# Softmax weights turned by DMA transposes for nine of twelve head pairs, and full-row norm matmuls

## The chip, the cores and the metric

The kernel runs on one core of a Trainium2 chip. The metric is the device time of one execution in microseconds (us), the median of several runs. The engines are named as the profile names them: PE (TensorE; PEld is its weight load), DVE (VectorE), ACT (ScalarE), POOL (GpSimd) and SP (SyncE, from whose queue all DMA transfers are issued).

## The reference

Causal attention, then a gated layer, then a second layer with two products. All arrays are float32.

```python
# q, k, v: (2, 12, 448, 64)
scores = q @ k^T / 8, masked above the diagonal
attn = softmax(scores)                       # max subtracted, sum + 1e-9
x = (attn @ v), heads joined                 # (896, 768)
xn = x / sqrt(mean(x * x) + 1e-6) * rms_g
x = (silu(xn @ w_gate) * (xn @ w_val)) @ w_out      # d_ff 1536
a, b = x @ w1, x @ w2                        # 1024 wide
return ((a * b) @ w3) @ w_out2               # (896, 768)
```

## The kernel before

**The plan.** The kernel does not issue its instructions as it builds them. Every piece of work is given to `add` (line 75) with an engine, a planned cost in us, the keys that it reads and writes, and a priority; some carry an alternative engine (`alt`). `schedule` (line 104) is a list scheduler with these costs: it holds the time at which each of PE, ACT, DVE, POOL and SP comes free, takes at each step the ready work of best priority, and lets the first free of the allowed engines have it. `order` (line 209) runs it eight times, each time with priorities taken from a schedule of the same work backwards, and keeps the shortest plan. The instructions are then issued in the plan's order, and each engine runs its own in that order. The constants at the top (TP, WP0, PO and so on, BIAS, THETA) are first priorities and the willingness to hand work to another engine. A DMA is planned as time on SP plus 2.0 us until it has landed (`LAT`).

**The stages.** Attention works on twelve pairs of heads (`pair`, line 525; six per batch, `p` counts them from 0 to 11). Beside it PE computes W' = w3 times the last weights (`w_prime`, line 487), 384 matmuls of 384 columns which only the last stage needs. After each batch comes `norm` (line 651). The layers after it use seven block products instead of eight (`wino`, line 777), on operands split into a float16 high part and a bfloat16 rest ("hi" and "lo"), with three matmuls per product of two split operands. Their weights arrive through `fetch` (line 446) and are split by `halve` (line 468).

**One pair.** The scores of two heads go to PSUM, four token tiles of 128, 128, 128 and 64 rows; `soft` (line 550) has DVE add the mask and find the maximum (line 552) and ACT take the exponential (line 556). The weights of tiles 0 to 2 lie in `pA`, one buffer of 128 x 768 float32 per head, those of the last tile of both heads in `pB` (128 x 512). For the product with the values they must lie the other way round, and split. That is `turn` (line 587): four PE transposes of 128x128 float32 into one PSUM bank (line 592), an ACT copy of the bank to float16 (line 595), and a DVE subtraction that leaves the rest as bfloat16 (line 597). Three turns fill `tA`, one fills `tB`: four turns a pair, 48 in all. Then `pv` (line 614) multiplies the turned parts with the split values, three matmuls of 65 or 64 columns per block, and DVE scales the result by the reciprocal sum into `x4s` (line 638). The buffers: `qs` three, `pA` three, `pB` two, `tA` and `tB` two each; weight loads (`st`) four.

**The norm.** DVE multiplies the identity by each token's factor (`diag`, line 661). For each of six head pairs, PE multiplies `x4` by it (line 672): three token tiles of 128 rows, and the last with only its 64 rows. An ACT copy with the gain follows (line 677), then the splitting.

The splitting helpers are `hi_part` (line 437: a copy on ACT, or else DVE or POOL) and `lo_part` (line 442: a subtraction on DVE, or else POOL). The PE matmuls of all stages stand on line 482.

Of the kernel before, what the change touches and what calls it, by code (L numbers as in the profile page):

```python
# [9 lines left out]
F16 = mybir.dt.float16  # L10
BF16 = mybir.dt.bfloat16
# [29 lines left out]
TP = 17.8003  # L41
WP0 = -253.0822
WPS = 51.892
GVS = 4.2731
OS = 5.0631
AS = 4.1976
FS = -1.7478
PO = dict(dq=71.6219, dv=1.9008, vh=22.6565, vl=32.9822, sc=-23.6522, s3=-41.3333, hA=-61.8192, hl=29.4612,
    hB=-32.8733, pv=17.37, sq=-46.6736, nm=20.7661, wm=29.3375, ww=-33.8468, wx=26.0812, g=-0.9384,
    a=-36.9422, o=12.4298, f=-33.5642, gm=-18.8521, e=9.4561, ae=-40.4366, y=-26.7884, t1=30.9235,  # L50
    mx=16.587, dw=4.4531)
# [3 lines left out]
BIAS = {"dve": 16.6032, "pool": 54.8731, "act": 110.9515}  # L55
THETA = 0.4938
# [216 lines left out]
def fused_kernel(ctx: ExitStack, tc, qk, v, g, wgv, wo, wab, w3t, wout, out):  # L273
# [82 lines left out]
    vl_r = Ring("att", "vl", 2, [P, NT * GH, D], F16)  # L356
    zero = view("zero", [P + 252], F16)
# [123 lines left out]
    def mm(*a, **k):  # L481
        nc.tensor.matmul(*a, **k)  # L482
# [42 lines left out]
    def pair(b, gi):  # L525
# [33 lines left out]
        def scores(i, outs, keys, pr):  # L559
# [7 lines left out]
            add("pe", (2 if i < 3 else 1) * (0.1 + w * 0.00082), f, r=[kqs], w=keys, prio=pr, rows=0.5)  # L567
# [19 lines left out]
        def turn(blocks, dst, kd, r, pr):  # L587
# [5 lines left out]
            add("pe", 4 * 0.109, f, r=["ident", *r], w=[kp], prio=pr)  # L593
# [6 lines left out]

        order = [(i, j, kb) for i in range(3) for j in range(GH) for kb in range(i + 1)]
        where = {x: c for c, x in enumerate(order)}
        for c in range(0, 12, 4):
# [3 lines left out]
        turn([pB[:, kb * P:kb * P + P] for kb in range(4)], [tB[:, h, :, 0:P] for h in range(2)], ktB, [kpB], t0 + PO["hB"])  # L607

        for j in range(GH):
# [4 lines left out]
            def pv(i, o=o, j=j):  # L614
                n = 3 * (i + 1)
                k = 0
                for kb in range(i + 1):
                    if i < 3:
                        c = where[i, j, kb]
                        lh, ll = tA[:, 0, c], tA[:, 1, c].bitcast(BF16)  # L620
# [7 lines left out]
            for i in range(NT):  # L628
                kt = {ktA + (where[i, j, kb] // 4,) for kb in range(i + 1)} if i < 3 else [ktB]
                add("pe", 3 * (i + 1) * 0.0286, lambda pv=pv, i=i: pv(i), r=[  # L630
                    *(k + (h,) for k in sorted(kt) for h in range(2)), kvh, kvl], w=[ko], prio=pr)
# [19 lines left out]
    def norm(b):  # L651
# [13 lines left out]
        for gi in (0, 3, 1, 4, 2, 5):  # L665
# [3 lines left out]
            def f(x4=x4, ps=ps):  # L669
                for i in range(NT):  # L670
                    n = ROWS[i]
                    mm(ps[:, i * P:i * P + n], x4[:n, i], diag[:n, i, :n], start=True, stop=True)

            add("pe", 4 * S / 2400.0, f, r=["diag"] + [kx4 + (j,) for j in range(GH)], w=[kp], prio=pr)
# [256 lines left out]
```

## Time and profile before

| | |
|---|---|
| median of 3 runs | 555.97 us (555.76 to 556.53) |
| the profiled execution | 554.84 us |
| its span, first to last instruction | 553.1 us |
| PE busy | 539.6 us (98%) |
| DVE busy | 497.6 us (90%) |
| ACT busy | 343.0 us (62%) |
| POOL busy | 232.8 us (42%) |
| mean granted clock of PE | 0.996 |

The profile is one execution, taken by the hardware profiler. An engine's busy time counts its instructions and not its waiting. PE's matmuls are pipelined and their ends are modelled, so a busy PE is not PE at its peak. The chain of waits starts at the last instruction and goes back, at each step, to what released it, or to the instruction before it on its engine.

### The profile page before, as it was taken

Reading aid. Unit: us, or ns where it says so; the run is one execution under the profiler, and the core shown is the slowest. Engines: PE = TensorE matmul, PEld = TensorE weight load, DVE = VectorE, ACT = ScalarE, POOL = GpSimd, SP = SyncE. Lnnn points to the kernel's source line nnn. Section 1 sums busy time; section 2 is a strip of 40 time slices with the busy share of each in tenths; the row PEclk is TensorE's granted clock in tenths of the full one; section 3 lists DMA queues with packets and bytes.
Section 4 is the critical chain, followed back from the end, with each engine's and each line's share of the span. In section 5 each row is a group of like instructions: output and inputs, shape, how many; then the busy total and the mean of one; then the engine's idle time right before and its main releaser. Section 6 shows DMA issues by size and latency. Waiting matters only on the chain.

```text
span 553.1 us, 9446 instructions
## 1 busy us (share of the span) xinstructions
PE 539.6 (98%) x3586; PEld 304.0 (55%) x3586; DVE 497.6 (90%) x919; ACT 343.0 (62%) x500; POOL 232.8 (42%) x198
## 2 busy tenths in 40 slices
PE   7799999999999999999999999999999999999997
PEld 5465666677667555555555555555555555455553
DVE  6898999889987999999999999999659999999943
ACT  5898869778755767676746677857435516533310
POOL 5545225164120475569674744132112476353300
PEclk8999999999999999999999999999999999999999
DMA  8887646723130232535231447536103311000121
GB/s 278 272 281 245 181 136 180 259 89 94 32 115 1 65 118 104 173 109 176 97 132 60 120 165 253 204 116 228 58 0 119 111 59 58 0 1 0 42 92 69
DMA packets 17470, 67.59 MB, mean 122 GB/s; under 512 B 2064, under 2 KB 3600, under 8 KB 17424
## 3 DMA queue, kind: packets, MB, share of 16 engines
q1 hardware_dynamic: 17424, 66.99, 36.3%
q8 instruction: 28, 0.46, 0.3%
q14 instruction: 18, 0.15, 0.1%
HBM read 64.23 MB, written 2.75 MB: 121 GB/s over the span
## 4 chain that ended last, share of the span: by engine, by line
PE 75%; DVE 15%; DMA 4%; issue 3%; ACT 2%; SPq 0%; DVEq 0%; ACTq 0%
PE bank L482 71%; PE bank L592 3%; DVE arena L443 3%; DMA st<-in_w3t 3%; DVE arena L795 3%; DVE arena L478 2%; DVE st L478 2%; DVE cv L464 2%; DVE cv L457 1%; DMA arena<-in_qk 1%; ACT st L460 1%; DVE arena L552 1%; PE bank L428 1%; DVE arena L439 0%; DVE st L462 0%
## 5 line engine op out<-in xcount | busy, mean ns | idle before, releaser
L482 PE MATMUL bank<-arena 128*128 128x448 f16 (+8 forms) x2976 | 446.2, 316 | 8.0 <-DVE arena L552 2.1
L482 PEld LDWEIGHTS <-arena 128*128 128x128 f16 x3048 | 250.8, 98 | 215.2 <-issue 11.6
L460 ACT ACTIVATE st<-st 128x768 uint16<-128x768 uint16 (+2 forms) x73 | 119.7, 1665 | 26.7 <-DVE cv L457 23.4
L795 DVE TENSOR_TENSOR arena<-bank,arena 128x448 f32<-128x448 f32 x161 | 92.6, 612 | 13.9 <-PE bank L482 13.3
L444 POOL TENSOR_TENSOR arena<-cv,arena 128x384 bf16<-128x384 f32 (+2 forms) x42 | 61.5, 1468 | 44.8 <-ACT arena L438 43.9
L444 POOL TENSOR_TENSOR arena<-arena 128x448 bf16<-128x448 f32 x32 | 51.2, 1613 | 65.1 <-ACT arena L438 65.0
L464 DVE SCALAR_TENSOR_TENSOR cv<-st,cv 128x768 int32<-128x768 int32 (+2 forms) x84 | 75.5, 905 | 1.8 <-ACT st L460 1.4
L482 PE MATMUL bank<-xs,arena 128*128 128x448 f16 x360 | 72.5, 352 | 0.0
L438 ACT ACTIVATE arena<-arena 128x448 f16<-128x448 f32 x73 | 40.6, 573 | 38.6 <-DVE arena L478 33.1
L457 DVE TENSOR_SCALAR cv<-st 128x768 int32<-128x768 int32 (+2 forms) x84 | 54.4, 654 | 8.0 <-DMA st<-in_w3t 4.1
L438 ACT ACTIVATE arena<-cv 128x384 f16<-128x384 f32 (+2 forms) x56 | 37.3, 673 | 29.8 <-PE bank L482 16.6
L443 DVE TENSOR_TENSOR arena<-st,arena 128x1536 bf16<-128x1536 f32 (+1 forms) x25 | 45.8, 1834 | 0.0
L478 DVE TENSOR_TENSOR arena<-arena 128x448 f32<-128x448 f32 x60 | 39.3, 667 | 6.9 <-ACT arena L841 4.5
L556 ACT ACTIVATE arena<-arena 128x256 f32<-128x256 f32 (+3 forms) x84 | 42.0, 519 | 5.5 <-DVE arena L552 5.3
L440 POOL TENSOR_SCALAR arena<-cv 128x384 f16<-128x384 f32 (+2 forms) x26 | 21.5, 828 | 55.8 <-DVE cv L464 28.4
L552 DVE CUSTOM_DVE_ANT_0 arena<-bank,arena 128x128 f32<-128x128 f32 (+3 forms) x84 | 36.3, 443 | 3.3 <-PE bank L482 2.5
L438 ACT ACTIVATE arena<-st 128x1536 f16<-128x1536 f32 (+1 forms) x21 | 29.0, 1383 | 15.4 <-DVE st L478 9.2
L597 DVE TENSOR_TENSOR arena<-bank,arena 128x512 bf16<-128x512 f32 x48 | 32.7, 684 | 6.2 <-ACT arena L595 6.0
L443 DVE TENSOR_TENSOR arena<-cv,arena 128x768 bf16<-128x768 f32 (+2 forms) x42 | 35.0, 833 | 0.9 <-POOL arena L440 0.7
L595 ACT ACTIVATE arena<-bank 128x512 f16<-128x512 f32 x48 | 29.0, 607 | 10.9 <-PE bank L592 10.5
L479 POOL TENSOR_TENSOR arena<-arena 128x448 f32<-128x448 f32 x20 | 27.5, 1378 | 16.0 <-DVE arena L795 14.7
L482 PEld LDWEIGHTS bank<-arena 64*128 64x128 f32 (+2 forms) x288 | 26.0, 179 | 14.9 <-issue 4.7
(69 smaller groups left out, 359.9 us busy)
## 6 DMA issues: line engine op xcount, KB each, us to landing
st<-in_wgv SPq DMA_DIRECT2D x24, 768.0 KB, 4.3
st<-in_wab SPq DMA_DIRECT2D x16, 768.0 KB, 4.7
st<-in_wo SPq DMA_DIRECT2D x12, 768.0 KB, 4.5
st<-in_w3t SPq DMA_DIRECT2D x16, 512.0 KB, 5.1
st<-in_wout SPq DMA_DIRECT2D x16, 384.0 KB, 3.5
arena<-in_qk SPq DMA_DIRECT2D x12, 448.0 KB, 4.4
arena<-in_v SPq DMA_DIRECT2D x12, 256.0 KB, 3.2
out_t<-arena SPq DMA_DIRECT2D x12, 224.0 KB, 1.9
```

Source lines behind the costliest of these rows:

```text
L438: add("act", act_us(n), lambda: nc.scalar.activation(hi, src, AF.Copy), r=r, w=w, prio=prio, alt=(("dve", dve2_us(n), lambda: nc.vector.te ...
L443: add("dve", dve_us(n), lambda: nc.vector.tensor_tensor(lo, src, hi, op=ALU.subtract), r=r, w=w, prio=prio, port=True, alt=(("pool", pool_ ...
L444: port=True, alt=(("pool", pool_us(n), lambda: nc.gpsimd.tensor_tensor(lo, src, hi, op=ALU.subtract)),))
L457: add("dve", dve2_us(n), lambda: nc.vector.tensor_scalar(cv, hi, 3, 0x3FFFFFFF, op0=ALU.logical_shift_left, op1=ALU.bitwise_and), r=[ks], ...
L460: add("act", ACT_TOP * n - 0.08, lambda: nc.scalar.activation(b[:, :, 2], b[:, :, 1], AF.Copy, scale=1.0 / 8192, bias=-8191.0 / 16384), w= ...
L464: add("dve", dve_us(n), lambda: nc.vector.scalar_tensor_tensor(cv, hi, -0x3FFFFFF9, cv, op0=ALU.bitwise_and, op1=ALU.bitwise_or), r=[ks], ...
L478: add("dve", dve_us(n), lambda: nc.vector.tensor_tensor(out, a, b, op=op), port=True, alt=(("pool", pool_us(n) + 0.1, lambda: nc.gpsimd.te ...
L482: nc.tensor.matmul(*a, **k)
L552: add("dve", dve_us(w), lambda: nc.vector.tensor_tensor_reduce(out=sc[:, :w], in0=ss[:, :w], in1=m, scale=-CSC, scalar=3.0e38, op0=ALU.add ...
L556: add("act", act_us(w) + 0.1, lambda: nc.scalar.activation(dst, sc[:, :w], AF.Exp, bias=mx[:, c:c + 1], scale=-1.0), r=[ksc, kmx + (c,)], ...
L597: add("dve", dve_us(512), lambda: nc.vector.tensor_tensor(dst[1].bitcast(BF16), src, dst[0], op=ALU.subtract), r=[kp, kd + (0,)], w=[kd + ...
L795: add("dve", dve_us(S), lambda: nc.vector.tensor_tensor(dst, ps, y, op=ALU.add), r=[kp, ky], w=[kd], prio=p)
```

## The change

Pairs 3 to 11 (`DA` for the three tiles of A, `DB` for the last tile) no longer turn their weights on PE. The weights are split first, as they lie: `hi_part` and `lo_part` write a float16 and a bfloat16 half side by side into a new buffer (`hA`, two of 128 x 2 x 768; `hB`, one of 128 x 2 x 512), and one DMA transpose on the SP queue turns both halves into `tA` or `tB`. That is three transfers a pair: one for A per head (768 columns, two halves), one for B (512 columns, two halves). Pairs 0 to 2 keep the four turns on PE. The order of the blocks in `tA` differs for the new way, so `pv` takes other indices and waits for other keys.

The norm's last token tile is multiplied over all 128 rows of `x4` and `diag`; the rows from 64 on meet zeros of `diag`.

The planned PE costs of scores, turns and the norm are changed, and the constants of the first priorities, BIAS and THETA have new values (in part left out below), so the order of the whole program can differ.

```diff
-TP = 17.8003
-WP0 = -253.0822
-WPS = 51.892
+TP = 28.0521
+WP0 = -244.6493
+WPS = 48.9793
...
-BIAS = {"dve": 16.6032, "pool": 54.8731, "act": 110.9515}
-THETA = 0.4938
+BIAS = {"dve": 17.4016, "pool": 80.0945, "act": 139.3857}
+THETA = 0.4843
+
+DA, DB = range(3,12), range(3,12)
...
+    hA_r = Ring("att", "hA", 2, [P, 2, 768], F16)
+    hB_r = Ring("att", "hB", 1, [P, 2, 512], F16)
...
-            add("pe", (2 if i < 3 else 1) * (0.1 + w * 0.00082), f, r=[kqs], w=keys, prio=pr, rows=0.5)
+            add("pe", 0.12 + 2 * (0.1 + w * 0.00082), f, r=[kqs], w=keys, prio=pr, rows=0.5)
...
-            add("pe", 4 * 0.109, f, r=["ident", *r], w=[kp], prio=pr)
+            add("pe", 4 * 0.109 + 0.04, f, r=["ident", *r], w=[kp], prio=pr)
...
+        def send(n, h, kh, src, ks, dst, kd, us, pr):
+            hi_part(n, h[:, 0], src, ks, [kh + (0,)], pr)
+            lo_part(n, h[:, 1].bitcast(BF16), src, h[:, 0], ks + [kh + (0,)], [kh + (1,)], pr + PO["hl"])
+            add("sp", us, lambda: nc.sync.dma_start_transpose(out=dst, in_=h.rearrange("p a c -> p (a c)")),
+                r=[kh + (0,), kh + (1,)], w=kd, prio=pr - 30)
+
         order = [(i, j, kb) for i in range(3) for j in range(GH) for kb in range(i + 1)]
         where = {x: c for c, x in enumerate(order)}
-        for c in range(0, 12, 4):
+        blk = tA.rearrange("p h c n -> p (h c) n")
+        for j in range(GH if p in DA else 0):
+            send(768, *hA_r.next(), pA[j][0], [pA[j][1] + (i,) for i in range(3)], blk[:, j * 12:j * 12 + 12],
+                 [ktA + (c, j) for c in range(3)], 1.8, t0 + PO["hA"])
+        for c in range(0, 0 if p in DA else 12, 4):
             turn([pA[j][0][:, OFF[i] + kb * P:OFF[i] + kb * P + P] for i, j, kb in order[c:c + 4]],
...
-        turn([pB[:, kb * P:kb * P + P] for kb in range(4)], [tB[:, h, :, 0:P] for h in range(2)], ktB, [kpB], t0 + PO["hB"])
+        if p in DB:
+            send(512, *hB_r.next(), pB, [kpB], tB.rearrange("p h c n -> p (h c) n")[:, :, 0:P],
+                 [ktB + (h,) for h in range(2)], 1.4, t0 + PO["hB"])
+        else:
+            turn([pB[:, kb * P:kb * P + P] for kb in range(4)], [tB[:, h, :, 0:P] for h in range(2)], ktB, [kpB], t0 + PO["hB"])
...
-                    n = ROWS[i]
-                    mm(ps[:, i * P:i * P + n], x4[:n, i], diag[:n, i, :n], start=True, stop=True)
-
-            add("pe", 4 * S / 2400.0, f, r=["diag"] + [kx4 + (j,) for j in range(GH)], w=[kp], prio=pr)
+
+                    mm(ps[:, i * P:i * P + ROWS[i]], x4[:, i], diag[:, i, :ROWS[i]], start=True, stop=True)
+
+            add("pe", 4 * S / 2400.0 + 0.03, f, r=["diag"] + [kx4 + (j,) for j in range(GH)], w=[kp], prio=pr)
```

## Rows read from the trace of the kernel before

**Rows 1.** The page's busy row: us (share of the span) xinstructions of each engine.

```profile
PE 539.6 (98%) x3586; PEld 304.0 (55%) x3586; DVE 497.6 (90%) x919; ACT 343.0 (62%) x500; POOL 232.8 (42%) x198
```

**Rows 2.** Chain of waits: 56.53 to 150.86 us by line; single pieces (start, us).

```profile
by line: PE bank L482 80.5%; PE bank L592 19.5%
...
42.95 5.68 DMA st<-in_w3t
...
56.53 0.44 PE bank L592 x4
...
150.41 0.45 PE bank L592 x4
...
164.75 8.69 PE bank L482 x56
...
193.75 230.01 PE bank L482 x1215
```

**Rows 3.** Stretches: length; busy of PE, PEld, DVE, ACT, POOL; clock, DMA share, GB/s.

```profile
0.00:52.50 52.50, 45.27 (x367) 28.84 (x368) 42.05 (x112) 40.81 (x62) 28.09 (x44) 0.97 0.81 267
52.50:150.40 97.90, 97.90 (x1026) 64.91 (x1026) 88.79 (x271) 78.67 (x159) 34.13 (x40) 1.00 0.46 146
150.40:194.00 43.60, 42.10 (x327) 27.33 (x325) 37.92 (x65) 27.26 (x56) 12.02 (x6) 1.00 0.18 60
194.00:424.00 230.00, 230.00 (x1218) 118.95 (x1217) 216.63 (x304) 149.99 (x168) 109.03 (x74) 1.00 0.38 131
```

**Rows 4.** The same table for the transposes of line 592 alone.

```profile
8.00:52.50 44.50, 6.23 (x40) 4.57 (x40) 0.96 0.83 271
```

**Rows 5.** Groups by shape: busy us, mean ns of one | idle before.

```profile
L595 ACT ACTIVATE arena<-bank 128x512 f16<-128x512 f32 x48 | 29.0, 607 | 10.9 <-PE bank L592 10.5
...
L443 DVE TENSOR_TENSOR arena<-cv,arena 128x768 bf16<-128x768 f32 x23 | 23.4, 1015 | 0.8 <-POOL arena L440 0.7
...
L438 ACT ACTIVATE arena<-cv 128x768 f16<-128x768 f32 x23 | 19.4, 842 | 9.6 <-DVE cv L464 8.4 <-PE bank L482 1.1
L444 POOL TENSOR_TENSOR arena<-cv,arena 128x768 bf16<-128x768 f32 x9 | 19.1, 2126 | 13.0 <-ACT arena L438 12.9
L444 POOL TENSOR_TENSOR arena<-cv,arena 128x512 bf16<-128x512 f32 x12 | 14.7, 1225 | 14.1 <-ACT arena L438 13.6
```

**Rows 6.** Single lines: duration ns min/median/max, first and last start.

```profile
L597 DVE TENSOR_TENSOR arena<-bank,arena x48: 660/684/693, 17.6 to 156.4; 128x512 bf16<-128x512 f32 x48
...
L443 DVE TENSOR_TENSOR arena<-arena x50: 606/616/1465, 171.4 to 512.9; 128x448 bf16<-128x448 f32 x50
...
L444 POOL TENSOR_TENSOR arena<-arena x32: 1035/1357/5788, 183.6 to 504.0; 128x448 bf16<-128x448 f32 x32
```

**Rows 7.** The page's DMA issues: xcount, KB each, median us to landing.

```profile
st<-in_wgv SPq DMA_DIRECT2D x24, 768.0 KB, 4.3
...
st<-in_wout SPq DMA_DIRECT2D x16, 384.0 KB, 3.5
...
arena<-in_v SPq DMA_DIRECT2D x12, 256.0 KB, 3.2
out_t<-arena SPq DMA_DIRECT2D x12, 224.0 KB, 1.9
```

**Rows 8.** Timeline of the SP queue: start, us, issue.

```profile
91.30 0.33 SPq L455 DMA_DIRECT2D st<-in_wgv  x1
...
122.17 0.33 SPq L455 DMA_DIRECT2D st<-in_wgv  x1
```

**Rows 9.** Groups of weight loads by shape, 167.4 to 180 us (second norm).

```profile
L482 PEld LDWEIGHTS bank<-arena 128*128 128x128 f32 x36 | 4.6, 191 | 0.4
...
L482 PEld LDWEIGHTS bank<-arena 64*128 64x128 f32 x12 | 1.8, 184 | 0.7
```

**Rows 10.** Timeline of weight loads around one last score tile: start, us.

```profile
105.28 0.19 PEld L482 LDWEIGHTS bank<-arena 64*64 64x64 f32 x4 [0.32 <-DVE arena L552]
106.17 0.42 PEld L592 LDWEIGHTS bank<-arena 128*128 128x128 f32 x4 [0.70 <-DVE arena L661]
```

More of the change, by code (lines that the diff above doesn't have):

```diff
@@ L37 @@
 CSC = 1.0 / 8.0
-TP = 17.8003
-WP0 = -253.0822
-WPS = 51.892
[L44 to L51, printed above, removed]
+TP = 28.0521
+WP0 = -244.6493
+WPS = 48.9793
+GVS = 6.4864
+OS = 3.1806
+AS = 4.3573
+FS = -5.7914
+PO = dict(dq=86.1608, dv=18.1427, vh=-4.1615, vl=31.153, sc=-23.1187, s3=-45.5392, hA=-61.1976, hl=15.902,
+    hB=-24.2123, pv=19.2543, sq=-20.7221, nm=29.1952, wm=26.8125, ww=-36.4818, wx=25.6973, g=24.6307,
+    a=-40.6597, o=14.4327, f=-41.7402, gm=-30.163, e=10.5623, ae=-45.2952, y=-25.9701, t1=23.8236,
+    mx=19.799, dw=-6.0874)
 PASSES = 8
-BIAS = {"dve": 16.6032, "pool": 54.8731, "act": 110.9515}
-THETA = 0.4938
+BIAS = {"dve": 17.4016, "pool": 80.0945, "act": 139.3857}
+THETA = 0.4843
+DA, DB = range(3,12), range(3,12)
 SQ = ({4: (0, 5, 0), 5: (5, 1, 1)}, {0: (0, 1, 0), 4: (1, 4, 1), 5: (5, 1, 2)})
@@ L619, in pv @@
                         c = where[i, j, kb]
-                        lh, ll = tA[:, 0, c], tA[:, 1, c].bitcast(BF16)
+                        if p in DA:
+                            c = j * 12 + OFF[i] // P + kb
+                        lh, ll = blk[:, c], blk[:, c + (6 if p in DA else 12)].bitcast(BF16)
                     else:
@@ L629, in pair @@
                 kt = {ktA + (where[i, j, kb] // 4,) for kb in range(i + 1)} if i < 3 else [ktB]
+                kt = [k + (h,) for k in sorted(kt) for h in range(2)]
+                if i < 3 and p in DA:
+                    kt = [ktA + (c, j) for c in range(3)]
                 add("pe", 3 * (i + 1) * 0.0286, lambda pv=pv, i=i: pv(i), r=[
-                    *(k + (h,) for k in sorted(kt) for h in range(2)), kvh, kvl], w=[ko], prio=pr)
+                    *kt, kvh, kvl], w=[ko], prio=pr)
             rs, krs = rs_r.next()
```

## The prediction

> **What bounds the kernel now.** I read the busy row of the page first: PE is busy for 539.6 of 553.1 us, DVE for 497.6, ACT for 343, POOL for 233 [rows 1]. A share over the whole span does not say where PE sets the pace, so I read the chain of waits next and cut the span where the chain changes hands: at 52.5, 150.4, 194 and 424 us. Up to 52.5 us the chain runs through loads, DVE and ACT (one load of in_w3t alone holds it for 5.68 us). From 56.5 to 150.9 us it never leaves PE. From there to 193.75 us it goes mostly through DVE and ACT, with two pieces of PE, and then it stays on PE for 230 us without a break [rows 2]. The table by stretch says what the others do meanwhile. In the second stretch (52.5 to 150.4 us, most of the attention) PE is busy for all of its 97.9 us and DVE for 88.8, ACT for 78.7, POOL for 34.1, the DMA engines for 0.46 of it. In the fourth, PE is full and DVE is at 94% [rows 3]. The reader is to see two things: PE time taken out of the second stretch is worth its full length, and DVE stands only 9.1 us of idle time behind PE there. The granted clock is 1.00 in that stretch, the upper of its two levels (2.4 GHz), so no part of the sum is a clock.
>
> **The change part by part.**
>
> *Turns off PE.* One turn is four f32 transposes in a row. The chain between 56.53 and 150.86 us (94.33 us) holds 37 of them (35 pieces, two of them double), with 19.5% of the time: 18.4 us, or 0.497 us each [rows 2]. Each pair has four turns (three of A, one of B); the change takes them from pairs 3 to 11, 36 of 48. Ten turns (40 transposes) lie before 52.5 us [rows 4], and twelve stay; so two of the chain's 37 stay, and 35 go: 35 x 0.497 = 17.4 us. The last of the 36 comes where the chain has left PE and counts as nothing (bound: 0.5 us gained).
>
> *What replaces the eviction.* A turn was emptied by an ACT copy of 512 columns (607 ns) and a DVE subtraction out of PSUM (684 ns) [rows 5, 6]. Now the same 2,048 columns a pair are split before they are turned: two hi copies of 768 and one of 512, and the same for lo, all out of SBUF. The 35 turns are 8.75 pairs. Removed: DVE 35 x 0.684 = 23.9 us, ACT 35 x 0.607 = 21.2. Added for hi on ACT: 842 ns for 768, and 607 for 512 (that of the old copy), 2 x 0.842 + 0.607 = 2.29 us a pair, 20.0 in all; so ACT goes from 78.7 to 77.5 us. Added for lo: on DVE 2 x 1.015 + 0.684 = 2.71 us a pair, 23.7 in all; on POOL 2 x 2.126 + 1.225 = 5.48 us a pair, 48.0 in all [rows 5]. The planner may choose either. I take half and half: DVE 88.8 - 23.9 + 11.9 = 76.8 us, POOL 34.1 + 24.0 = 58.1. Bounds: all on DVE 88.6; all on POOL, DVE 64.9 and POOL 82.1.
>
> The stretch would be 97.9 - 17.4 = 80.5 us. DVE now has 9.1 us of idle time beside its work, in which it waits for scores and copies. With as much again it takes 76.8 + 9.1 = 85.9, so the stretch gives back 5.4 us. Bounds: nothing (DVE with 3.7 us of idle), and 17.2 us (all lo on DVE, 88.6 + 9.1 = 97.7). I take 5.4.
>
> A subtraction out of PSUM takes 660 to 693 ns whatever else runs. One of two SBUF inputs takes 606 ns at best and 1,465 at worst, on POOL 1,035 and 5,788 [rows 6]. The Trainium skill (SBUF — State Buffer, Who interferes with whom) says why that may be: a DVE instruction with two SBUF inputs and a GpSimd instruction that reads SBUF block each other, one with a single SBUF input does not. The spread in rows 6 agrees; by that rule the change moves 36 subtractions from the undisturbed kind to the disturbed one, which makes the larger give-back likelier. The prices above are means that hold the disturbance as it is now.
>
> *The sends.* 27 transfers of 384 KB (18) and 256 KB (9) go out on the SP queue, each after its lo. Plain loads of these sizes land in 3.5 and 3.2 us, the smallest store in 1.9, one of 768 KB in 4.3 [rows 7]. I take 3.5, bounds 1.9 and 4.3 as long as turning costs what moving does. A pair's path from weights to values becomes hi, lo, send (0.84 + 1.0 to 2.1 + 3.5 = 5.4 to 6.5 us) instead of turn, copy, subtraction (0.5 + 0.61 + 0.68 = 1.8). What hides it are matmuls of other pairs and of W', which need none of it: cost 0. Without that cover, the value matmuls stand at the head of PE's queue and hold all behind them: 4.7 us for each uncovered pair. On SP an issue takes 0.33 us [rows 8], 27 of them 9 us; a send that waits for its lo holds the qk, v and weight loads queued behind it, which are issued ahead of use (qk in three buffers, weights in four). Taken as 0, bounded by one 4.7 us stall.
>
> DMA time: nine pairs send 9.44 MB. The stretch moves 146 GB/s at a share of 0.46, so 317 GB/s at full share [rows 3], and the sends take 29.8 us, 29.0 of them there. With the loads (0.46 x 97.9 = 45.0) that is 74.0 of 80.5 us: nearly full, not over.
>
> *Norm.* Six groups of the second norm: loads of 128 rows 4.6 us and 0.4 idle before them (36), of 64 rows 1.8 us and 0.7 idle (12) [rows 9]. As full-row loads the 12 would cost 12/36 x 4.6 = 1.5, and the 1.1 us of changing between the two kinds would go: 1.4 us for six groups, 2.7 for twelve. Some ten of the twelve lie in chain pieces on PE (the first norm inside the stretch, four groups of the second in the piece at 164.75 us [rows 2]): 2.3 us. Bounds: 0, and 4.8 (all of the 64-row time and idle).
>
> *Scores, turn and norm costs, offsets.* These change only the planner's order. The last score tile was planned at 0.1 + 448 x 0.00082 = 0.47 us; from its weight load to the next one the trace has 0.89 [rows 10]; the new figure is 1.05. Better figures can help where PE waits, which it does for 1.5 us in the third stretch and 7.2 in the first [rows 3]. I take 0, bounds 4 us either way, since the order of the first loads is free to move too.
>
> *Sum.* 17.4 + 2.3 - 5.4 = 14.3 us off the profiled execution's 554.84 (span 553.1 and 1.7 around it): 540.5. The median of the runs is 1.1 higher, 555.97: **541.7**.
>
> **The rivals.**
>
> *PE gets all of it.* POOL takes most of lo and nothing is given back: 555.97 - 19.7 = 536.3, and with the norm's upper bound and the last turn 533.3. For it: POOL idles 63.8 us in the stretch [rows 3]. Against: a POOL subtraction costs twice DVE's.
>
> *The vector engines keep it.* All lo stays on DVE, or the two block each other as much: 17.2 us given back, 2.5 left, 553.5. For it: 91% of DVE in the stretch now, 94% in the fourth, so the work cannot go later. Against: the planner sees POOL idle.
>
> *Sends too slow: slower than before.* No transfer in this trace turns anything. If turning costs more DMA time than moving, the stretch is full of DMA: 45.0 + 29.0 f us at f times the price, less the wgv loads that can move out (six, issued between 91.30 and 122.17 us [rows 8], 2.5 us each, 15). The gain is gone where 30 + 29.0 f = 97.9, so from f = 2.3; at three times the price the stretch takes 117 us, 19 more than now, which with the norm's 2.3 gives 572.7. For it: nothing shows the price. Against: the bytes are those of plain loads. The Trainium skill stands on both sides. VectorE: DVE Perf Modes (The three transpose paths) gives 1,309 ns for one 128x128 block by DMA against 390 by TensorE; by that figure, taken per block, my estimate is 377 us for the sends and a kernel far slower. DMA: Bandwidth & Descriptors (Latency and other measured facts) gives 261 GB/s for a DMA transpose of scattered rows; by that the estimate is 36 us, and it would fit. No run here shows either.
>
> **How the numbers follow.** Forecast (537.5 to 549) 0.55; PE gets all (533 to 537.5) 0.18; the vector engines keep it (549 to 556) 0.14; slow sends (over 557) 0.13. A difference under 0.2% (1.1 us) can't be told from none here. Faster is all but the edge of the third and all of the fourth: 0.85; same 0.03; slower 0.12. The range leaves out the fourth and the ends of the others: 533 to 555.
>
> **What would show it.** Right: L592 falls from 192 to 48 transposes; the attention's end moves some 14 us earlier at full PE; the sends land in about 3.5 us; POOL is busier by over 20 us; the norm has no 64-row loads. The forecast is wrong if PE's value matmuls wait for a DMA for more than 2 us a pair, or if DVE in the attention shows no idle time at all while PE does.

## The result, and the profile after

The kernel after takes 550.05 us (median of 4 runs, 548.47 to 552.78) against 556.25 for the kernel before beside it (555.76 to 556.77). The ratio is 0.9894, with a 95% interval from 0.9852 to 0.9935. It is faster, as forecast, and inside the whole range of 533 to 555 us, but by 6.2 us where 14.3 were forecast. It lies outside the forecast's own interval (537.5 to 549), in that of the second rival (549 to 556), which had a chance of 0.14. The PE time was taken out, and some two thirds of it was given back, in two places. The profiled execution is the fastest of the four (548.47 us), with a mean granted clock of PE of 1.000; that of the kernel before had 0.996.

The busy row of the kernel after (the same form as [rows 1]):

```profile
PE 524.3 (96%) x3442; PEld 286.6 (52%) x3442; DVE 495.8 (91%) x909; ACT 338.8 (62%) x492; POOL 237.5 (43%) x198
```

PE is busy 15.3 us less, but the span shrank by 6.4 us only (553.1 to 546.7). The stretches of the kernel after answer to [rows 3]; the second is cut 9.0 us earlier, just behind its last exponential (140.8 us in place of 149.7), the fourth has the same 230 us:

```profile
52.50:141.40 88.90, 84.83 (x885) 50.17 (x882) 82.05 (x244) 73.99 (x144) 49.34 (x48) 1.00 1.05 232
...
182.00:412.00 230.00, 226.18 (x1190) 115.85 (x1189) 216.22 (x311) 141.22 (x166) 86.51 (x65) 1.00 0.37 127
```

The reader is to see three things. PE is no longer full in either: 4.1 us of idle time in the second, 3.8 in the fourth. The DMA share of the second went from 0.46 to 1.05. POOL does 15.2 us more in the second and 22.5 less in the fourth. The chain of waits says what PE waits for (start, us, what; the longest pieces):

```profile
79.78 4.90 DMA arena<-arena
...
94.98 4.27 DMA arena<-arena
...
129.66 6.92 DMA arena<-arena
138.52 5.82 DMA arena<-arena
146.64 6.85 DMA arena<-arena
...
159.47 22.62 PE bank L486 x142
183.37 2.40 DVE cv L468
...
250.89 42.74 PE bank L486 x225
...
310.48 151.33 PE bank L486 x799
```

In the attention five sends hold the chain for 28.8 us, where it never left PE before. And in the gated layer the chain goes through DVE, in pieces of one to three us, from 183 to 250 us and again around 300, where before it stayed on PE for 230 us from 193.75 [rows 2].

One row dates both losses, and it is used for every run below: the matmuls that read the normed activations (`xs`), from the first start to the last. First the kernel before, then the kernel after:

```profile
L482 PE MATMUL bank<-xs,arena x360: 352/352/363, 179.6 to 494.7; 128*128 128x448 f16 x120, 128*128 128x448 bf16 x60
```

```profile
L486 PE MATMUL bank<-xs,arena x360: 349/352/363, 168.7 to 489.4; 128*128 128x448 f16 x120, 128*128 128x448 bf16 x60
```

The gated layer begins 10.9 us earlier, but takes 320.7 us where it took 315.1. So of some 20 us of PE work taken out of the attention 10.9 us arrive at its end, and 5.6 of those are lost again behind it; 5.3 are left at the last of these matmuls, 6.4 at the end of the span.

A little of the 10.9 us is the clock. Over the first 52.5 us the granted clock was 0.97 in the kernel before [rows 3] and 1.00 in the kernel after. Two kernels below, x7_unit512 and x15_split, have the attention of the kernel after and had 0.97 there; they begin the gated layer at 169.7 and 169.9 us. So my estimate is that about 1 of the 10.9 us comes from the clock.

The sends themselves (durations on the SP queue in ns, min/median/max; who waited, us and times; landing):

```profile
L608 SPq DMA_TRANSPOSE arena<-arena x27: 1231/1527/4877, 69.0 to 148.0; - x27
...
  PEld L486: 3.2, 7
  ACT arena L442: 2.9, 4
  POOL arena L444: 2.9, 3
  PE bank L486: 0.9, 3
...
DMA to landing us min/median/max: 3.1/5.4/7.5
```

The waits on ACT and POOL are those of hi copies whose buffer a send still reads. In sum the 27 sends hold the SP queue for 52.9 us.

And who splits what, by shape, from 55 to 150 us (busy us, mean ns of one, idle before):

```profile
L447 DVE TENSOR_TENSOR arena<-arena 128x768 bf16<-128x768 f32 x16 | 17.4, 1090 | 1.5 <-POOL st L483 0.8 <-ACT arena L442 0.7
...
L448 POOL TENSOR_TENSOR arena<-arena 128x512 bf16<-128x512 f32 x5 | 6.2, 1239 | 5.3 <-ACT arena L442 5.2
...
L447 DVE TENSOR_TENSOR arena<-arena 128x512 bf16<-128x512 f32 x4 | 4.2, 1046 | 0.4 <-ACT arena L442 0.4
...
L448 POOL TENSOR_TENSOR arena<-arena 128x768 bf16<-128x768 f32 x2 | 3.5, 1772 | 0.4 <-ACT arena L442 0.4
```

20 of the 27 lo parts stay on DVE, 7 go to POOL.

### The profile page after: what moved, and what is told of

The parts are those of the page before. It is cut to its first block, busy times and chain, and to the rows that moved or that the text cites. A ratio compares the mean times of both kernels' runs of the same rounds, so it can differ in the third digit from the quotient of the medians.

```text
span 546.7 us, 9215 instructions
## 1 busy us (share of the span) xinstructions
PE 524.3 (96%) x3442; PEld 286.6 (52%) x3442; DVE 495.8 (91%) x909; ACT 338.8 (62%) x492; POOL 237.5 (43%) x198
## 4 chain that ended last, share of the span: by engine, by line
PE 54%; DVE 23%; DMA 8%; issue 5%; ACT 3%; POOL 0%; DVEq 0%; SPq 0%; ACTq 0%
PE bank L486 54%; DVE arena L818 6%; DVE arena L447 6%; DMA arena<-arena 5%; DVE cv L468 3%; DVE st L482 3%; DVE cv L461 2%; DVE arena L482 2%; DMA st<-in_wout 2%; ACT st L464 1%; DMA st<-in_w3t 1%; DVE arena L556 1%; ACT arena L442 1%; ACT arena L560 1%; DVE arena L547 0%
## 5 line engine op out<-in xcount | busy, mean ns | idle before, releaser
L486 PE MATMUL bank<-arena 128*128 128x448 f16 (+10 forms) x2976 | 446.1, 315 | 14.7 <-ACT wpr L516 3.9
L442 ACT ACTIVATE arena<-arena 128x448 f16<-128x448 f32 (+2 forms) x90 | 53.9, 612 | 40.4 <-DVE arena L482 27.8
L448 POOL TENSOR_TENSOR arena<-arena 128x448 bf16<-128x448 f32 (+2 forms) x29 | 49.6, 1713 | 56.7 <-ACT arena L442 44.5
L447 DVE TENSOR_TENSOR arena<-arena 128x448 bf16<-128x448 f32 (+2 forms) x80 | 61.2, 780 | 2.4 <-ACT arena L442 1.1
L442 ACT ACTIVATE arena<-cv 128x768 f16<-128x768 f32 (+2 forms) x61 | 41.0, 679 | 32.5 <-DVE cv L468 18.6
L448 POOL TENSOR_TENSOR arena<-cv,arena 128x384 bf16<-128x384 f32 (+2 forms) x31 | 44.4, 1434 | 24.8 <-ACT arena L442 24.2
L560 ACT ACTIVATE arena<-arena 128x384 f32<-128x384 f32 (+3 forms) x84 | 41.2, 518 | 5.8 <-DVE arena L556 5.2
L447 DVE TENSOR_TENSOR arena<-cv,arena 128x768 bf16<-128x768 f32 (+2 forms) x53 | 43.3, 824 | 0.8 <-POOL arena L444 0.7
L442 ACT ACTIVATE arena<-st 128x1536 f16<-128x1536 f32 (+1 forms) x22 | 30.5, 1389 | 17.4 <-DVE st L482 7.7
L556 DVE CUSTOM_DVE_ANT_0 arena<-bank,arena 128x384 f32<-128x384 f32 (+3 forms) x84 | 35.7, 441 | 1.9 <-PE bank L486 1.2
L815 ACT ACTIVATE arena<-bank 128x448 f32<-128x448 f32 x23 | 12.6, 546 | 25.3 <-PE bank L486 15.2
```

Of the source, the lines that this page charges most:

```text
L442: add("act", act_us(n), lambda: nc.scalar.activation(hi, src, AF.Copy), r=r, w=w, prio=prio, alt=(("dve", dve2_us(n), lambda: nc.vector.te ...
L447: add("dve", dve_us(n), lambda: nc.vector.tensor_tensor(lo, src, hi, op=ALU.subtract), r=r, w=w, prio=prio, port=True, alt=(("pool", pool_ ...
L448: port=True, alt=(("pool", pool_us(n), lambda: nc.gpsimd.tensor_tensor(lo, src, hi, op=ALU.subtract)),))
L556: add("dve", dve_us(w), lambda: nc.vector.tensor_tensor_reduce(out=sc[:, :w], in0=ss[:, :w], in1=m, scale=-CSC, scalar=3.0e38, op0=ALU.add ...
L560: add("act", act_us(w) + 0.1, lambda: nc.scalar.activation(dst, sc[:, :w], AF.Exp, bias=mx[:, c:c + 1], scale=-1.0), r=[ksc, kmx + (c,)], ...
```

## The experiments

Twelve kernels were run, each timed beside the kernel before. The table holds what they gave: the ratio to the kernel before with its interval, and from the row of `xs` the start and length of the gated layer.

| run | median us | ratio [95%] | gated start | its length |
|---|---|---|---|---|
| before | 555.3 to 556.4 | 1 | 179.6 | 315.1 |
| after | 550.05 | 0.9894 [0.9852, 0.9935] | 168.7 | 320.7 |
| x4_norm | 552.84 | 0.9934 [0.9917, 0.9951] | 175.5 | 317.0 |
| x3_turn1 | 549.70 | 0.9885 [0.985, 0.992] | 171.6 | 315.3 |
| x12_turn1_lo | 545.54 | 0.9831 [0.9787, 0.9875] | 169.5 | 315.2 |
| x1_plain | 549.86 | 0.9882 [0.9851, 0.9913] | 171.4 | 320.2 |
| x2_lo32 | 548.27 | 0.9858 [0.9829, 0.9888] | 171.0 | 320.2 |
| x8_nowait | 548.74 | 0.9868 [0.9841, 0.9895] | 170.8 | 320.7 |
| x13_nowait_plain | 549.30 | 0.9898 [0.9862, 0.9935] | 170.7 | 320.3 |
| x6_plain_lo32 | 543.32 | 0.9767 [0.9742, 0.9793] | 164.3 | 320.7 |
| x11_all | 540.95 | 0.973 [0.9703, 0.9757] | 159.1 | 320.8 |
| x7_unit512 | 544.95 | 0.9789 [0.9758, 0.9821] | 169.7 | 315.8 |
| x15_split | 556.72 | 1.0016 [0.9991, 1.0041] | 169.9 | 323.4 |
| x10_pe | 565.25 | 1.0167 [1.0139, 1.0195] | 177.8 | 326.7 |

The starts come from one profiled execution each, and these differ in the granted clock. Over the first 52.5 us it was 1.00 in after, x4_norm and x11_all, 0.97 in before, x3_turn1, x12_turn1_lo, x8_nowait, x13_nowait_plain, x7_unit512 and x15_split, 0.93 in x1_plain, x2_lo32 and x10_pe, and 0.90 in x6_plain_lo32. So this column alone does not tell apart starts that differ by 2 or 3 us. The times carry the clock too: the six runs of x3_turn1 took 550.5 to 553.9 us at mean granted clocks of 0.986 to 0.990, and 547.1 to 548.9 us at 0.997.

### The parts alone, in the order of before

**x4_norm**: only the norm's instruction of the change.

```diff
-                    n = ROWS[i]
-                    mm(ps[:, i * P:i * P + n], x4[:n, i], diag[:n, i, :n], start=True, stop=True)
+                    mm(ps[:, i * P:i * P + ROWS[i]], x4[:, i], diag[:, i, :ROWS[i]], start=True, stop=True)
```

> The kernel before with the norm's last token tile over all 128 rows, order as before. By the prediction's step 2.3 us less, 554. Theory V: part of it is given back in the gated layer, 1 to 1.5 us less, 555. In both, a group of the second norm takes about 1.0 us of PE instead of 1.22.

3.5 us by the medians (2.7 to 4.6 by the ends of the interval). The weight loads of the second norm in the kernel after (158 to 170 us) answer to [rows 9]: all of 128 rows, 5.6 us with their idle time where there were 7.5, so 1.9 for six groups and 3.8 for twelve.

```profile
L486 PEld LDWEIGHTS bank<-arena 128*128 128x128 f32 x48 | 5.5, 192 | 0.1
```

**x3_turn1**: three of four transposes left out in the turns of pairs 3 to 11, and nothing put in their place.

```diff
-                for c, x in enumerate(blocks):
+                for c, x in enumerate(blocks[:1] if p >= 3 else blocks):
```

> The kernel before with one transpose instead of four in each turn of pairs 3 to 11 (108 of 192 are left out, so three quarters of what is copied from the bank is old); everything else and the order as before. No DMA is added and DVE, ACT and POOL have the same work, so this is the PE time alone. By the prediction's step (PE time taken out of the second stretch is worth its full length): 108 x 0.124 = 13.4 us, 543. Theory V: the gated layer starts 9 to 13 us earlier and gives a third to a half of it back, 547 to 550.

6.7 us by the medians (some 9 by its runs at a granted clock of 0.997, near which most runs of the kernel before stood), and the gated layer starts 8.0 us earlier, for 13.4 us of transposes left out (36 turns, three quarters of the prediction's 0.497 us each). So even with no send the attention keeps some 5 us: DVE's work is as before (84.78 of the 88.9 us up to 141.4), and 3.9 us of PE's weight loads wait for the subtractions of line 597. The gated layer, in its old order, takes as long as before, and its chain stays on PE for 149 of the 154 us from 181 to 335 us.

```profile
52.50:141.40 88.90, 87.47 (x922) 54.08 (x921) 84.78 (x262) 75.60 (x158) 34.05 (x40) 1.00 0.49 161
```

```profile
by line: PE bank L482 97.0%; DVE arena L443 1.2%; DVE cv L464 1.1%; DVE arena L795 0.4%; DVE arena L478 0.3%; DVE st L478 0.3%; issue 0.0%
...
185.72 149.41 PE bank L482 x789
```

**x12_turn1_lo** takes from that kernel three quarters of the subtraction behind those turns as well.

```diff
+            m = 1 if p >= 3 else 4
             add("dve", dve_us(512), lambda: nc.vector.tensor_tensor(
-                dst[1].bitcast(BF16), src, dst[0], op=ALU.subtract), ...
+                dst[1][:, :m].bitcast(BF16), src[:, :m], dst[0][:, :m], op=ALU.subtract), ...
```

> The kernel before with one transpose of four in the turns of pairs 3 to 11, as x3_turn1, and with the subtraction behind each of these turns over 128 instead of 512 columns (the rest of lo is old), which takes 36 x 0.4 = 14 us more from DVE, in the order of the kernel before. By the prediction's term (DVE needs 9.1 us of idle time beside its work, and that took 5.4 of the 13.4 us back): the gated layer starts at 166 to 168 us instead of 171.6, and the time is 543 to 546 instead of 549.7. If DVE's total is not what takes it back: no more than 1.5 us of change.

4.2 us less than x3_turn1 by the medians, 3.0 by the ratios (the intervals just overlap), and 2.3 where both had a granted clock of 0.997. The start moves by 2.1 us to 169.5, not to the 166 to 168 of the first theory. DVE relief is worth something in the attention, but does not bring all 13.4 us.

### The sends: one load at a time, then in pairs

**x1_plain** makes plain copies of the sends, so the turning is left out; **x2_lo32** splits lo of the sends over 32 columns only; **x8_nowait** lets the value matmuls of pairs 3 to 11 read blocks that no send writes. In x8_nowait the hi copies still wait for the send that reads their buffer (ACT 4.0 us, POOL 2.2).

```diff
-            add("sp", us, lambda: nc.sync.dma_start_transpose(out=dst, in_=h.rearrange("p a c -> p (a c)")),
+            add("sp", us, lambda: nc.sync.dma_start(out=dst, in_=h.rearrange("p a c -> p (a c)").rearrange("p (k n) -> p k n", n=P)),
```

```diff
-            lo_part(n, h[:, 1].bitcast(BF16), src, h[:, 0], ks + [kh + (0,)], [kh + (1,)], pr + PO["hl"])
+            lo_part(n, h[:, 1].bitcast(BF16), src, h[:, 0], ks + [kh + (0,)], [kh + (1,)], pr + PO["hl"], 32)
...
```

```diff
+                        if p in DA:
+                            sl = slice((c - j * 12) * P, (c - j * 12) * P + P)
+                            lh, ll = w3[j][:, 0, sl], w3[j][:, 1, sl].bitcast(BF16)
...
```

> The changed kernel with its 27 sends as plain copies of the same bytes between the same buffers, in the same order; the turning itself is left out, so the weights reach the values unturned. Theory D (the turning costs the DMA engines twice what moving does, so sends and loads land late and PE waits): the share of DMA time falls by some 30 us, the sends land in 3.5 us or less, the first product of the gated layer starts at 163 us or earlier instead of 168.7, and the time is 543 to 546. Theory V (DVE is the second bound, in the attention and after it): the gated layer starts at 167 to 169 and the time stays within 1.5 us of 550.

> The changed kernel with the lo subtractions of the sends over 32 columns instead of 768 or 512 (the rest of lo is left out, set to zero once at the start), transposes and order as they are. That takes about 20 us from DVE and 7 from POOL. Theory V: DVE gets ahead again, the gated layer loses less than 1.5 us of the lead with which it starts (4.7 of 10.9 now), and the time is 541 to 545. Theory D: sends still land in over 5 us, PE goes on waiting, and the time is 548 to 550.

> The changed kernel, but the value matmuls of pairs 3 to 11 read blocks of w3 that have long been in SBUF instead of the turned weights; the splits and the sends run as before, only nobody waits for them (the turned weights are left out of the result). Theory L (the longer way from weights to values, hi, lo and a send that lands in 5.4 us, makes PE wait in its fixed order): PE's waits in the attention go, the gated layer starts 5 to 8 us earlier than in the changed kernel, and the time is 543 to 546. Theory O (the new order costs it: PE waits for scores, banks and DVE there, and not for sends): less than 2 us, 548 to 551.

None of the three moved the time by more than 1.8 us, and none can be told from the kernel after by its interval. Each theory that expected the gain from one load alone was wrong. Then all of them were taken away together, with hi cut to 32 columns too.

**x11_all**: the three edits above, and

```diff
-            hi_part(n, h[:, 0], src, ks, [kh + (0,)], pr)
+            hi_part(n, h[:, 0], src, ks, [kh + (0,)], pr, 32)
...
```

> The changed kernel with all that the sends add made small at once: hi and lo over 32 columns, the sends as plain copies, and the value matmuls of pairs 3 to 11 reading blocks of w3, so that nobody waits for a send (the splits of these pairs, the turning and its use are left out). Theory S (the small loads that the sends add on ACT, DVE, POOL and DMA act together, so that no single one shows): the gated layer starts at 164 us or earlier, where the changed kernel and the three runs before started at 168.7 to 171.4, and the time is 542 to 546. Theory O (what is left is the attention's own chain through DVE and ACT in this order): the start stays at 167 us or later, 546 to 550.

540.95 us, 9.1 less than the kernel after, and the gated layer starts at 159.1 us: 20.5 us earlier than before, all of the PE time that the change takes out. So the loads of the sends cost the attention its 10 us, but not one by one. Two more kernels looked for the pair: **x13_nowait_plain** (x8_nowait with plain copies) and **x6_plain_lo32** (x1_plain with lo over 32 columns).

> The kernel after, in which the sends are plain copies and the value matmuls of pairs 3 to 11 read the joined blocks that the second kernel of the wait test reads, so that nobody waits for a send (the weights are not the turned ones: the outputs are not the reference's). hi and lo stay as they are. Each of these two alone moved the time by 0.2 and 1.3 us; with hi and lo cut to 32 columns as well it fell by 9.1. Theory S1 (the DMA price and the waiting cover each other: take away both and the relief comes): 541 to 544 us, first start of the gated layer's matmuls at about 161 us. Theory S2 (the vector work of hi and lo is needed for it as well): 547 to 549 us, that start at about 170 us.

> The kernel after with plain copies for the sends and with their lo over 32 columns only (the outputs are not the reference's): the DMA price and half of the vector work go, hi and the waiting stay. Theory S1 (the DMA price and the waiting are the pair that covers each other): 547 to 549 us, as with lo alone. Theory S2 (vector work and DMA price together): 542 to 545 us, first start of the gated layer's matmuls at about 163 us in place of 168.7.

Taking the waiting of the value matmuls away together with the DMA price of turning changed nothing that shows (549.3 us). Taking away that price together with the subtractions did: 543.32 us, 6.7 of the 9.1.

The start of x6_plain_lo32 in the table, 164.3 us, looks late because this execution was already behind before the first send, at the clock of 0.90. The same exponential, some 10 us before the first send, in the kernel after, in x6_plain_lo32 and in x11_all (start, us):

```profile
58.17 0.96 ACT L560 ACTIVATE arena<-arena 128x448 f32<-128x448 f32 x2
```

```profile
61.29 0.96 ACT L564 ACTIVATE arena<-arena 128x448 f32<-128x448 f32 x2
```

```profile
57.17 0.96 ACT L566 ACTIVATE arena<-arena 128x448 f32<-128x448 f32 x2
```

From there to the gated layer it is 110.5 us in the kernel after, 103.0 in x6_plain_lo32 and 101.9 in x11_all: the pair brings 7.5 of the 8.6 us. With one load gone, or with plain copies and no waiting, it is 110.6 to 111.7 us, no gain at all.

The stretch from 60 to 160 us shows why. Columns as in [rows 3]; the kernel after, then with plain copies, with lo cut, with both, and with all four loads gone:

```profile
60.00:160.00 100.00, 93.50 (x1016) 56.52 (x1017) 89.80 (x254) 81.47 (x163) 57.73 (x53) 1.00 1.05 229
```

```profile
60.00:160.00 100.00, 94.07 (x1017) 57.27 (x1016) 89.76 (x257) 79.98 (x155) 54.61 (x50) 0.98 0.72 233
```

```profile
60.00:160.00 100.00, 93.82 (x1021) 57.05 (x1020) 74.75 (x261) 80.79 (x158) 40.10 (x51) 0.98 1.08 233
```

```profile
60.00:160.00 100.00, 97.97 (x1068) 60.33 (x1067) 76.69 (x267) 85.01 (x169) 45.54 (x56) 1.00 0.74 238
```

```profile
60.00:160.00 100.00, 98.57 (x1087) 62.52 (x1086) 75.39 (x265) 78.51 (x175) 39.81 (x55) 1.00 0.73 232
```

Plain copies bring the DMA share from 1.05 to 0.72 and leave DVE at 89.8: PE is at 94.1 in place of 93.5. lo cut brings DVE to 74.8 and leaves the DMA at 1.08: PE at 93.8. Only both together free PE (98.0). The chains of waits from 55 to 160 us name the limit that is left each time, here of the kernel after, of plain copies, of lo cut, and of both:

```profile
by line: PE bank L486 29.9%; DMA arena<-arena 27.4%; DMA st<-in_wout 8.2%; issue 5.2%; DVE arena L447 4.8%; DVE arena L556 4.0%; ACT arena L442 3.5%; ACT arena L560 3.3%; ACT st L464 2.3%; DVE arena L547 2.2%; DVE cv L461 2.2%; DVE cv L468 
```

```profile
by line: PE bank L486 37.6%; issue 13.6%; DVE arena L447 9.3%; DVE arena L556 8.2%; DMA arena<-in_v 4.8%; DMA st<-in_wout 4.3%; DVE cv L461 3.5%; ACT arena L560 3.1%; DVE cv L468 2.7%; ACT arena L442 2.6%; DVE arena L661 2.0%; ACT st L464 1
```

```profile
by line: PE bank L490 35.7%; DMA arena<-arena 25.5%; DMA st<-in_w3t 5.2%; issue 4.7%; ACT arena L564 4.6%; ACT arena L444 4.4%; DMA st<-in_wout 4.2%; DMA arena<-in_v 3.2%; DVE cv L465 2.9%; DVE arena L451 2.3%; ACT st L468 1.9%; ACT arena L
```

```profile
by line: PE bank L490 63.7%; ACT arena L564 5.0%; DMA arena<-arena 4.4%; issue 4.0%; DMA st<-in_wout 3.9%; ACT arena L444 3.6%; ACT st L468 2.8%; DVE arena L560 2.3%; DVE cv L472 2.0%; DVE cv L465 2.0%; ACT wpr L520 1.7%; DVE arena L451 1.4
```

With plain copies the chain goes through DVE (its subtractions, the scores' masks, the weights' conversions); with lo cut it passes sends for 25.5%; with neither it is on PE for 63.7%. Two limits of about the same height lie behind PE, and taking one away shows the other. What part of the sends' price it is stays open: plain copies lower their DMA time, their hold of the SP queue (from 52.9 us in sum to 15.2) and their landing (from 5.4 to 4.2 us) all at once, and lo cut together with the waiting was not tried.

### The gated layer

**x7_unit512**: the kernel after, with the 1,536-column subtraction of nine of the twelve gated units over 512 columns only.

```diff
-        halve(1536, flat(hi[:, 3:]), flat(lo[:, 3:]), flat(s), ks, ukey(r, 3), pr)
+        halve(1536, flat(hi[:, 3:]), flat(lo[:, 3:]), flat(s), ks, ukey(r, 3), pr, m)
...
-        unit(wgv[f], f % 3, pr + PO["g"])
+        unit(wgv[f], f % 3, pr + PO["g"], 512 if f > 2 else None)
```

> The changed kernel with the lo subtraction of the four weight sums over 512 instead of 1,536 columns for nine of the twelve weight units of the gated layer (the rest of lo is left over from an earlier unit), which takes some 9 us from DVE in that layer; the order is unchanged. Theory G (in the gated layer DVE is the bound in the new order, and takes back 4.7 us of the lead): the loss there falls below 1.5 us and the time is 546 to 547. Against it: no change, 550.

544.95 us, 5.1 less than the kernel after, and the gated layer is back at 315.8 us. From 200 to 320 us, first the kernel after, then this one:

```profile
200.00:320.00 120.00, 116.23 (x610) 59.07 (x609) 118.57 (x163) 75.01 (x89) 55.76 (x44) 1.00 0.38 126
```

```profile
200.00:320.00 120.00, 119.75 (x634) 61.87 (x633) 112.91 (x171) 77.07 (x91) 56.05 (x45) 1.00 0.41 138
```

DVE falls from 118.6 to 112.9 of 120 us and PE fills (116.2 to 119.75). The chain from 181 to 335 us, on PE for 44.5% in the kernel after, is here on PE for 77.6%:

```profile
by line: PE bank L488 77.6%; DVE arena L820 7.0%; DVE st L484 3.1%; issue 3.0%; DVE cv L470 2.9%; ACT st L466 2.8%; DVE cv L463 1.8%; DVE arena L449 1.2%; DVE arena L484 0.5%; ACT arena L442 0.2%; ACTq L466 0.0%
...
217.76 117.25 PE bank L488 x619
```

So DVE is the limit that costs the 5.6 us there. The loss goes with the new order of the work and not with the earlier start alone: x3_turn1 and x12_turn1_lo start 8.0 and 10.1 us earlier in the old order and lose 0.2 and 0.1; the kernels in the order of after whose gated layer is untouched lose 5.1 to 5.7, x11_all with its 20.5 us of lead as well as x1_plain with 8.2. The exception is x4_norm: in the old order too, it loses 1.9, and its chain from 181 to 335 us is on PE for 17.0% only, where that of the kernel before is for 91.7%. So the old order stands near the same limit; why x4_norm passes it is open.

One thing that the new plan did shows in the 448-column subtractions of lo during the gated layer, on DVE and on POOL, before (179.6 to 494.7 us) and after (168.7 to 489.4):

```profile
L443 DVE TENSOR_TENSOR arena<-arena 128x448 bf16<-128x448 f32 x36 | 23.6, 673 | 1.2 <-POOL arena L440 0.9 <-ACT arena L438 0.3
...
L444 POOL TENSOR_TENSOR arena<-arena 128x448 bf16<-128x448 f32 x30 | 48.5, 1631 | 56.1 <-ACT arena L438 55.9
```

```profile
L447 DVE TENSOR_TENSOR arena<-arena 128x448 bf16<-128x448 f32 x50 | 33.0, 677 | 0.5 <-POOL arena L444 0.5
...
L448 POOL TENSOR_TENSOR arena<-arena 128x448 bf16<-128x448 f32 x20 | 36.8, 1843 | 48.4 <-ACT arena L442 36.3 <-DVE arena L818 12.0
```

DVE has 14 more of them and POOL 10 fewer; in all, DVE is busy for 3.6 us more in these stretches (305.28 after 301.66) and POOL for 16.8 less (138.66 after 155.48). That fits the loss, but no run changed this division alone.

**x15_split** was the attempt at a better kernel, with nothing left out: POOL, idle for over half of that stretch, takes 512 of those columns beside DVE. The edit also reaches the same subtractions of the layer behind (19 in all).

```diff
...
+        def both():
+            nc.gpsimd.tensor_tensor(l[:, 1024:], x[:, 1024:], h[:, 1024:], op=ALU.subtract)
+            nc.vector.tensor_tensor(l[:, :1024], x[:, :1024], h[:, :1024], op=ALU.subtract)
...
```

> The kernel after, with nothing left out: where the plan gives the 1,536-column subtraction of a gated unit to DVE, DVE does 1,024 of the columns and POOL, idle for over half of that stretch, the other 512 beside it. Between 181 and 333 us ten of them take 1.749 us each on DVE; two thirds of it should take about 1.2, so DVE is relieved of 5.5 us, a little over half of what the kernel with 512 of 1,536 columns took off, which gained 5.1 us. Theory G (DVE is what holds the gated layer): 546.5 to 548.5 us, with DVE between 200 and 320 us at 115 of 120 us in place of 118.6. Rival (the two engines block each other when both read SBUF, so 1,024 columns on DVE take as long as 1,536 did): 549.5 to 551 us, with the 1,024 columns at 1.5 us or more.

556.72 us: slower than the kernel after by 6.7 us, further than the rival had said. Not all of that is the split. The gated layer is 2.7 us longer than in the kernel after, and 11 of the 12 runs had a mean granted clock of 0.987 to 0.994; the one at 1.000 took 552.23 us, where the kernel after took 548.47 at 1.000. Its window from 200 to 320 us, and the two halves (ns, min/median/max):

```profile
200.00:320.00 120.00, 114.05 (x593) 57.93 (x591) 119.05 (x160) 74.60 (x88) 78.30 (x54) 0.99 0.37 125
```

```profile
L778 DVE TENSOR_TENSOR arena<-st,arena x19: 1205/1214/2185, 144.3 to 484.7; 128x1024 bf16<-128x1024 f32 x19
```

```profile
L777 POOL TENSOR_TENSOR arena<-st,arena x19: 1155/1446/7296, 143.8 to 487.2; 128x512 bf16<-128x512 f32 x19
```

POOL did 22.5 us more and DVE was not relieved at all (119.05). 1,024 columns take 1.21 us at the median and up to 2.19, the 512 of POOL 1.16 us at best and up to 7.30. Nine of the smaller DVE halves take 13.6 us in that window, where nine whole ones took 15.7. But the 448-column subtractions beside them became longer, first in the kernel after, then in this one:

```profile
L447 DVE TENSOR_TENSOR arena<-arena 128x448 bf16<-128x448 f32 x10 | 6.5, 658 | 0.0
```

```profile
L447 DVE TENSOR_TENSOR arena<-arena 128x448 bf16<-128x448 f32 x10 | 9.2, 930 | 0.0
```

So the 2.1 us saved on DVE went into other DVE work while POOL was busier, in line with the spread in [rows 6].

### The order

**x10_pe** keeps the constants, planned costs and norm of after, and turns all 48 on PE.

```diff
-DA, DB = range(3,12), range(3,12)
+DA, DB = range(0), range(0)
```

> The changed kernel with all 48 turns on PE again (its planned costs, constants and norm stay). The difference to the changed kernel is what the sends are worth. By the prediction's sum (17.4 less 5.4 for the turns) 12 us slower than the changed kernel, 562. If what the sends free is mostly given back: 552 to 555, which is the norm's gain alone. The order is planned anew, so a few us may come from that alone.

565.25 us, 9.6 more than the kernel before, with 11.6 us more in the gated layer. It has an order of its own, neither that of before nor that of after, so this does not price the sends. It shows that the order can move this kernel by some 10 us, more than twice the 4 us that the prediction allowed it; a part of it may be the granted clock, 0.988 to 0.994 in its runs and 0.991 to 1.000 in those of the kernel before beside it.

## Why the direction was right and the size wrong

The forecast had the gated layer begin 14.3 us earlier and keep that lead to the end. It began 10.9 us earlier, 3.4 short; then 5.6 us were lost in the gated layer, and 1.1 came back behind it. Two steps failed, the second by more than the first: the give-back in the attention was taken too small, and the step "PE time taken out of the second stretch is worth its full length", with the cost of the new order put at 0, did not hold up to the end of the kernel. Neither of the two signs that should have shown the forecast wrong came; both looked at the attention only.

**PE time removed: right.** The transposes fall from 192 to 48. The chain between 56.53 and 150.86 us shows 34 pieces of them, two double, so 36 turns of 0.513 us and not 37 of 0.497; two of these stay and 34 go, which is 17.4 us again. x11_all shows that this PE time is worth its full length up to the gated layer when nothing takes its place: 20.5 us earlier (about 1 of it by the clock), against 17.4 + 2.3 = 19.7 in the sum.

**Norm: right in kind, 2.3 us forecast, 3.5 measured** (x4_norm), inside its bounds of 0 and 4.8.

**The give-back in the attention: mis-sized.** The forecast took 5.4 us, between bounds of 0 and 17.2; 9.6 were given back (20.5 us of lead in x11_all against 10.9 in the kernel after). Two of its inputs failed. Half of lo was to go to POOL, with DVE at 76.8 us and POOL at 58.1 in the stretch; 20 of 27 stayed on DVE, and they are at 82.05 and 49.34. DVE's idle time of 9.1 us beside its work was nearly right: 6.9. With DVE's real figure that rule gives 82.05 + 9.1 = 91.2 us for the stretch, where 88.9 were measured. But the rule knew one limit, and there were two: with lo cut (x2_lo32) the time hardly moved, because the sends were the next limit.

**The sends: priced too low, and the price not alone decisive.** They land in 5.4 us, not 3.5 (bounds 1.9 and 4.3). They hold the SP queue for 1.5 us each at the median and 52.9 us in all, not for 0.33 and 9. The queue's share of 16 engines' span, before and after:

```profile
q1 hardware_dynamic: 17424, 66.99, 36.3%
```

```profile
q1 hardware_dynamic: 55152, 76.43, 48.1%
```

263.0 less 200.8 is 62.2 us of DMA time for the sends, where 29.8 were forecast; as plain copies (41.1% of 548.9 us) they cost 24.8. So turning cost 2.1 times the forecast and 2.5 times moving. The rival of slow sends was right that turning costs more. Its sum at 2.1 gives 30 + 29.0 x 2.1 = 90.9 us for the stretch, near the measured 88.9, but not by its mechanism alone: the DMA share went over 1.0 (1.05 for 88.9 us), which its sum took for impossible, and plain copies alone, with the share back at 0.72, gained nothing. The Trainium skill's two figures (VectorE: DVE Perf Modes, The three transpose paths; DMA: Bandwidth & Descriptors, Latency and other measured facts) had given estimates of 377 us and 36 us; the trace has 62.2, nearer to the second.

**The cover: nearly right.** PE's value matmuls and their loads wait for sends for 0.9 + 3.2 us in all, far under the 2 us a pair that would have refuted the forecast, and x8_nowait gains 1.3 us by the medians. What the sends delay is the work queued beside them: the chain passes the sends for 27.4% between 55 and 160 us with hi, lo and the weights' loads and conversions between its pieces.

**The cost of the new order: taken as 0, bounded by 4 us, and 5.6 in the gated layer alone.** This is the step that failed most. The forecast carried the lead through the fourth stretch because PE was full there and DVE at 94% [rows 3]. In the new order DVE is the limit there: PE waits for it, and x7_unit512, which relieves DVE alone, returns 5.1 us. The second rival had named DVE's 94% in the fourth stretch as its reason, so the mechanism was on record, as a rival with a chance of 0.14. What in the new order makes DVE the limit was not settled; the 14 more subtractions on DVE fit it, and POOL beside DVE did not help in x15_split.

**The clock: taken as no part of the sum.** In the second stretch that held (1.00, the upper of the two levels). In the first the granted clock was 0.97 before and 1.00 after, which is worth about 1 us by the estimate above, in the change's favour. That is luck of the two executions compared.

**The shared path.** The rule of the Trainium skill (SBUF — State Buffer, Who interferes with whom: a DVE instruction with two SBUF inputs and a GpSimd one that reads SBUF block each other) fits x15_split, whose halves take up to 2.19 and 7.30 us, against 1.21 and 1.16 at best. It was counted for the larger give-back, and that came; no run shows that it came by this.

The sum with the measured terms: 20.5 - 9.6 - 5.6 = 5.3 us at the last `xs` matmul, 6.4 at the end of the span, 6.2 by the medians. The two losses are taken from the same rows as the result, so that this adds up is no test.

## What to carry to other kernels

Work taken from the bounding engine is worth its length only up to the next limit, and that is to be looked for in every stage up to the end: a lead won in one stage can be lost where another engine stands at 94%, above all if the order changes too. When taking away one suspected load changes nothing, take away two before clearing it: two limits of one height hide each other. An idle engine beside a full one is not a reserve for certain: here giving it a third of a subtraction made other work longer. And before two starts are compared, look at a point that the edit cannot have touched: here it already differed by up to 4.1 us.

## What the runs showed of the hardware that was not expected

- A DMA transpose from SBUF to SBUF costs DMA time and queue time: 9.44 MB took 62.2 us of 16 engines, 24.8 as plain copies, and one holds the SP queue for 1.23 to 4.88 us (52.9 us for the 27, and 15.2 as plain copies).
- The DMA share of a stretch can stand above 1 (1.05 for 88.9 us), so a sum of packet times up to the length of a stretch is no bound.
- Splitting one subtraction between DVE and POOL did not relieve DVE in the gated layer (119.05 of 120 us busy, 118.57 without the split) and held POOL for up to 7.30 us for 512 columns; 448-column subtractions of DVE beside it took 930 ns in place of 658.
- The time of one and the same kernel differs with the granted clock by more than most of the edits changed it: x3_turn1 took 547.1 to 548.9 us at a mean of 0.997 and 550.5 to 553.9 at 0.986 to 0.990.
